# Attention and two expert layers on one core: the routing inside a unit takes one more step, row splits come later, weight splits of the remainder unit are spread anew

## The chip, the cores and the metric

The kernel runs on one core of a Trainium2 chip. The metric is the time of one execution in microseconds of device time. A measurement of the kernel is the median over several runs.

## The reference

Three parts follow each other. First attention over 4 batches, 12 heads, 448 rows of 64, with normalised queries and keys. Its output, 1,792 rows of 768, goes through two layers of eight experts. A row goes to the expert with the largest logit, and the expert's output is scaled by the softmax weight of that expert (in the first layer also by a sigmoid gate). The second layer adds a bias by the row's modality to the logits.

```python
logits = x @ w_gate + modality_bias[modality_id]      # layer 2; layer 1 has no bias
e_idx = np.argmax(logits, axis=1)
gate_w = softmax(logits)[rows, e_idx]
for e in range(8):
    h = np.maximum(x[e_idx == e] @ w1[e], 0.0)        # 768 to 1,024
    out[e_idx == e] = gate_w * (h @ w2[e])            # 1,024 to 768
```

## The kernel before, in words

Attention fills about the first 320 us. Then the two layers are done as a list of **units**. A unit is one expert with a group of the rows that were routed to it. In layer 1 there are a first unit `ua` (240 columns), the remainder unit `ub` (128 columns, the same expert) and then `P0` to `P6`, with room for 304, 288, 256, 240, 224, 208 and 192 rows. Layer 2 follows with `e2` and `e3` (304 rows each) and the smaller remainder groups.

Every value is kept as a high and a low half, so a product is three matmuls. A unit (`unit`, `halves`) has eight **first-layer steps**, each 18 matmuls into one PSUM buffer `pl`, of which there are three. After each, ACT writes the high half `hh` and VectorE the low half `hl` of the hidden block (line 377); the buffer is free for another step when `hl` is done. Beside them the weights of the second layer are split, `w2h` on ACT and `w2l` on VectorE (line 305). Then come six **second-layer steps** of 24 matmuls, which read `hh` and `hl`, and after each a transposition and the scaled rows `yr` on VectorE (line 436). In these the first-layer weights of the next unit are split (`w1h`, `w1l`).

The function `do(s)` is called at each step s of a unit (0 to 7 first layer, 7.5 between, 8 to 13 second layer) and does what is not matmul work:

- the **row splits** of the next unit, by the table `XPLAN`: "p" splits tile t of the gathered rows `xr` into `XS`, the high half on ACT (line 356) and the subtraction on GpSimd (line 357), "s" does the subtraction on VectorE, "t" is the transposing DMA on SyncE's queue;
- the fetch of rows for the unit after the next;
- one step of the **generator of the unit before** (`gen`): at step 0 its last transposition, the scatters of its rows `yr` to the table `yd` (one GpSimd DMA for each tile of 128 rows, line 382) and the logits' copy `lt`; at step 1 the logits `r_l` (line 489) for layer 2's routing and the routing itself up to the one-hot rows `rt_ohb` (line 112), two steps later the rank matmuls `rk` (lines 121 to 124), one step later the rest of the routing;
- side work from a dictionary, such as the weight splits for `P0` in `ub`.

Each engine works through its instructions in the order in which they are written. The scatters of a unit to `yd` wait for each other: the second is issued when the first has landed.

Of the kernel before, what the change touches and what calls it, by code (L numbers as in the profile page):

```python
# [9 lines left out]
NT=1792; D=768; F=1024; E=8; KD=6; KF=8  # L10
# [17 lines left out]
class Moe:  # L28
# [60 lines left out]
    def apart(self,i,key):  # L89
        i=getattr(i,"ins",i)  # L90
        self.tc.declare_no_dep(i,group=key,reason="a token has one place: the scatters write different rows"); self.tc.add_to_no_dep_group(key,i)
    def route_g(self, sp, psp, l, nt, R, ohsum, ordt, tokf=None, valid=None, og=None, mod=None, tag="sm", pay=None, iv=None, fine=0, apart=None):

        nc=self.nc; V=nc.vector
        T=lambda n,s=(),dt=F32: sp.tile([128,nt,*s],dt,name="rt_"+n,tag="rt_"+n)[:R]
        m=T("m"); V.tensor_reduce(m,l,axis=AX.X,op=ALU.max)
        if fine: yield
        d=T("d",(E,)); V.tensor_tensor(out=d,in0=l,in1=bc(m.unsqueeze(2),[R,nt,E]),op=ALU.subtract)
        ex=T("ex",(E,)); nc.scalar.activation(ex,d,AF.Exp)
        if fine: yield  # L100
        v=T("v",(E,)); V.scalar_tensor_tensor(out=v,in0=d,scalar=0.0,in1=bc(self.e8m[:R].unsqueeze(1),[R,nt,E]),op0=ALU.is_ge,op1=ALU.mult)
        if fine: yield
        mn=T("mn"); V.tensor_reduce(mn,v,axis=AX.X,op=ALU.min)
        if fine: yield
        s=T("s"); V.tensor_reduce(s,ex,axis=AX.X,op=ALU.add)
        if fine: yield
        oh=T("oh",(E,)); V.tensor_tensor(out=oh,in0=bc(self.e8m[:R].unsqueeze(1),[R,nt,E]),in1=bc(mn.unsqueeze(2),[R,nt,E]),op=ALU.is_equal)
        if fine: yield
        if valid is not None:
            V.tensor_tensor(out=oh,in0=oh,in1=bc(valid.unsqueeze(2),[R,nt,E]),op=ALU.mult)  # L110
            if fine: yield
        ohb=T("ohb",(E,),BF16); V.tensor_copy(ohb,oh)
        if fine:
            yield
            smx=T("smx",(E,))[:,0]; V.tensor_reduce(smx,oh.rearrange("p t e -> p e t"),axis=AX.X,op=ALU.add)
            rk=(yield "rk").rearrange("p (t e) -> p t e",t=nt)
        else:
            yield
            yield
            rk=psp.tile([128,nt,E],F32,name="rk",tag=tag)[:R]  # L120
        nc.tensor.matmul(rk,self.ones[:R,:R],bc(ohsum[:R].unsqueeze(1),[R,nt,E]),start=True,stop=False)
        for t in range(nt-1):
            nc.tensor.matmul(rk[:,t+1:],self.ones[:R,:R],bc(ohb[:,t:t+1],[R,nt-1-t,E]),start=False,stop=False)
        nc.tensor.matmul(rk,self.tri[:R,:R],ohb,start=False,stop=True)
# [12 lines left out]
        V.tensor_tensor(out=r,in0=r,in1=oh,op=ALU.mult)
        if fine: yield
        ix=T("ix"); V.tensor_reduce(ix,r,axis=AX.X,op=ALU.add)
        if fine: yield  # L140
        ixi=T("ixi",(),I32)
        if iv is None and valid is not None: iv=T("iv"); V.tensor_scalar(iv,valid,-BIG,BIG,op0=ALU.mult,op1=ALU.add)
        if iv is not None: V.tensor_tensor(out=ixi,in0=ix,in1=iv,op=ALU.add)
        else: V.tensor_copy(ixi,ix)
        if fine: yield
        if pay is None:
            pay=T("pay",(PW,)); nc.gpsimd.memset(pay[:,:,2:4],0.0)
            V.tensor_copy(pay[:,:,0],tokf)
            if mod is not None: V.tensor_copy(pay[:,:,2],mod)
        den=T("den"); V.tensor_scalar(den,s,1e-9,None,op0=ALU.add)  # L150
        if fine: yield
        if og is not None:
            V.scalar_tensor_tensor(out=den,in0=eo,scalar=1.0,in1=den,op0=ALU.add,op1=ALU.mult)
            if fine: yield
        V.reciprocal(pay[:,:,1],den)
        for t in range(nt):
            if fine: yield "sc"
            i=nc.gpsimd.indirect_dma_start(out=ordt[:,:],out_offset=bass.IndirectOffsetOnAxis(ap=ixi[:,t:t+1],axis=0),in_=pay[:,t,:],in_offset=None,bounds_check=E*NT-1,oob_is_err=False)
            if apart is not None: self.apart(i,apart); self.places.append(getattr(i,"ins",i).name)
# [109 lines left out]
    def alloc_rows(self,st,NM):  # L269
        nc=self.nc; ntl=(NM+127)//128; self.NM=NM; self.ntl=ntl  # L270
        self.XT=st.tile([128,2,KD,NM],F16,name="XT"); self.xh=self.XT[:,0]; self.xl=self.XT[:,1].bitcast(BF16)
        self.XS=st.tile([128,ntl,2,D],F16,name="XS")
        self.xr=[st.tile([128,D],F32,name=f"xr{t}") for t in range(ntl)]
        self.pays=[st.tile([128,ntl,PW],F32,name=f"pay{i}") for i in range(4)]
        self.idxs=[st.tile([128,ntl],I32,name=f"idx{i}") for i in range(4)]
        self.post=None; self.slot=0; self.turn=0; self.places=[]
    def clear_rows(self,j):
        for p in [self.xr[j]]+(self.pays if j==0 else []): self.nc.gpsimd.memset(p,0.0)
# [63 lines left out]
    def fetch_idx(self,u):  # L342
        nc=self.nc; ntl=u.ntl; pay=self.pays[u.slot]; idx=self.idxs[u.slot]
        v=self.lp.tile([128,self.ntl],F32,name="fv")[:,:ntl]
        nc.vector.tensor_scalar(v,self.pos3[:,:ntl],u.ent.cnt[:,u.g:u.g+1],None,op0=ALU.is_lt)
        nc.vector.scalar_tensor_tensor(out=v,in0=pay[:,:ntl,0],scalar=float(-NT),in1=v,op0=ALU.add,op1=ALU.mult)
        nc.vector.tensor_scalar(idx[:,:ntl],v,float(NT),None,op0=ALU.add)
    def gather(self,u,t=None):
        nc=self.nc; ntl=u.ntl; idx=self.idxs[u.slot]
# [122 lines left out]
    def warm2(self,db,eng):  # L472
        for k in ((0,1),(2,),(3,),(4,),(5,),())[db]: self.split_w1(k,eng=eng if k in (1,3) else None)
    def route2(self, u, scale):
        nc=self.nc; R=128; nx=u.L.nxt; sp=self.lp; sm=self.sm; ntl=u.ntl; yt=self.yt; pay=self.pays[u.slot][:,:ntl]; idx=self.idxs[u.slot][:,:ntl]
        nc.scalar.copy(self.lt[:2*E,:u.N],self.lgp[:2*E,:u.N])
        yield
        lg=sm.tile([128,ntl,E],F32,name="lg2",tag="tp")
        for t in range(ntl): nc.tensor.matmul(lg[:,t,:],self.lt[:2*E,ts(t,128)],self.fold[:2*E],start=True,stop=True)
        T=lambda n,s=(),dt=F32: sp.tile([128,self.ntl,*s],dt,name="r2_"+n,tag="r2_"+n)[:,:ntl]  # L480
        l=T("l",(E,)); b=T("b",(E,)); b2=T("b2",(E,)); nm=T("nm"); v=T("v"); tok=T("tok")
        sh=[128,ntl,E]
        nc.vector.tensor_copy(tok,idx)
        nc.vector.tensor_scalar(v,tok,float(NT),None,op0=ALU.is_lt)
        nc.vector.tensor_scalar(nm,pay[:,:,2],-1.0,1.0,op0=ALU.mult,op1=ALU.add)
        nc.vector.tensor_tensor(out=b,in0=bc(nx["bias"][:,0:1,:],sh),in1=bc(nm.unsqueeze(2),sh),op=ALU.mult)
        nc.vector.tensor_tensor(out=b2,in0=bc(nx["bias"][:,1:2,:],sh),in1=bc(pay[:,:,2:3],sh),op=ALU.mult)
        nc.vector.tensor_tensor(out=b,in0=b,in1=b2,op=ALU.add)
        nc.vector.tensor_tensor(out=l,in0=lg,in1=bc(scale,sh),op=ALU.mult)
        nc.vector.tensor_tensor(out=l,in0=l,in1=b,op=ALU.add)  # L490
        yield from self.route_g(sp,sm,l,ntl,R,nx["ohsum"],nx["ord"],tok,valid=v,tag="tp")

XPLAN={5:{0:[("p",2)],1:[("t",0),("t",1),("t",2)]},7:{9:[("s",0),("t",0)]},4:{0:[("p",0)],2:[("t",0),("t",1),("t",2)]},6:{1:[("t",0),("t",1),("t",2)]},0:{0:[("p",0),("p",1),("p",2)],7.5:[("t",0),("t",1),("t",2)]},3:{3:[("s",0)],4:[("s",1)],5:[("s",2)],7.5:[("t",0),("t",1),("t",2)]},
1:{8:[("s",0),("s",1),("s",2),("t",0),("t",1),("t",2)]},
    2:{7.5:[("s",0),("s",1),("s",2),("t",0),("t",1),("t",2)]},None:{10:[("s",0),("t",0)]}}
class LazyUnit:
# [329 lines left out]
def body_full(tc,q,k,v,g_q,g_k,wg,wog,w1,w2,mod,wg2,bias2,v1,v2,out,stop=False,O=None):  # L826
    nc=tc.nc
    with ExitStack() as ctx:
# [8 lines left out]
        S={}  # L837
# [113 lines left out]
                next(S[name],None)  # L951
            return f
        def xp(t): return lambda: M.xsplit(S["P"][0],t,nc.gpsimd)
        def w1(k): return lambda: M.split_w1(k,u=S["P"][0])
        M.unit(ua,nx=LazyUnit(S,"ub",same=True),fx=LazyUnit(S,"P",0),side={0:[tail0,step],1:[step,step],2:[step],5:[tail2],6:[tail3],7.5:[lambda: M.fetch_rows(S["ub"])],12:[xp(0)],13:[xp(1)]},late=7,fp=7,fr=9)
        P=S["P"]
        M.unit(S["ub"],nx=P[0],fx=P[1],side={j:[w1(k)] for k,j in enumerate((2,3,4,5,8,9))},late=5,fr=9)
        off2=cst.tile([128,E],F32,name="of2")
        def pick2():
            yield from M.pick_g("p2",lp,tp,c2,N2,tag="tp")  # L960
# [7 lines left out]
        S["B"]=[Unit(L2,be,g,N2) for g in range(G2)]; S["S"]=[Unit(L2,se,g,NS,x=True) for g in range(2)]  # L968
        B0=S["B"][0]
        P+=[LazyUnit(S,"e2"),LazyUnit(S,"e3")]  # L970
        sides={1:{KF+j:[stepper("table1")] for j in range(6)},2:{5:[stepper("pick2")]*2,**{j:[stepper("pick2")] for j in range(6,14)}},3:{5:[stepper("pick3")]*2,**{j:[stepper("pick3")] for j in range(6,14)}}}
        for g in range(7): M.unit(P[g],nx=P[g+1],fx=P[g+2],side=sides.get(g),late=0 if g else 3)
        e2,e3=S["e2"],S["e3"]
        def cold(u): M.fetch(u); M.cold(u); M.xall(u)
# [87 lines left out]
```

## Time and profile before

| what | value |
|---|---|
| runs shown, median (lowest to highest) | 886.72 us (885.95 to 888.47), 3 runs |
| profiled execution, its own time | 888.97 us |
| its span | 887.2 us |
| mean granted PE clock | 0.973 of full |
| PE, VectorE, ACT, GpSimd busy | 823.5, 674.9, 525.8, 389.9 us |

Busy shares are means over the whole span; attention and the two layers have different limits. The profiled execution is one run, 2.25 us over the median of the runs shown.

### The profile page before, as it was taken

To read this page: it belongs to the slowest core of one execution; us is meant where nothing else is said; L and a number is where in the kernel's file an instruction comes from. 1 tells how busy PE (TensorE), PEld (TensorE's weight loads), DVE (VectorE), ACT (ScalarE), POOL (GpSimd) and SP (SyncE) were. 2 spreads that over 40 slices of the span, in tenths; PEclk is the share of its full clock that TensorE was granted. 3 is DMA by queue.
4 is the path that set the end of the run, shared out by engine and by line. 5 is a ranking of instruction groups with operands and counts; after the bars stand their busy time and mean duration, and the time that the engine had idled before them with its cause. 6 is when DMAs were issued, how large, how long until landed. Compare 5 with 4: busy or idle time off the path is not lost. (4 is left out here: it accounts for less than half of the span.)

```text
span 887.2 us, 23322 instructions
## 1 busy us (share of the span) xinstructions
PE 823.5 (93%) x8881; PEld 644.0 (73%) x8898; DVE 674.9 (76%) x1414; ACT 525.8 (59%) x967; POOL 389.9 (44%) x409
## 2 busy tenths in 40 slices
PE   4699999999999799799999999989999999989996
PEld 1365666666665588677889899889777778867775
DVE  6689889888878775775788888888775768558865
ACT  4577777776766653555555656666445545437653
POOL 5686777876776523420514333433402424023202
PEclk9799999999999899999999999999999999999999
DMA  5577666765565383959495797797778776967941
GB/s 135 128 159 192 153 157 159 198 158 155 130 172 127 124 238 84 332 196 279 144 323 146 271 302 190 265 347 166 268 243 288 233 187 250 279 211 237 346 158 51
DMA packets 142138, 181.44 MB, mean 204 GB/s; under 512 B 71944, under 2 KB 109592, under 8 KB 142016
## 3 DMA queue, kind: packets, MB, share of 16 engines
q1 hardware_dynamic: 134048, 157.06, 60.3%
q0 software_dynamic: 6656, 22.32, 7.9%
q8 instruction: 72, 1.18, 0.6%
q10 hardware_dynamic: 1312, 0.47, 0.2%
q14 instruction: 50, 0.41, 0.1%
HBM read 129.73 MB, written 23.94 MB: 173 GB/s over the span
## 5 line engine op out<-in xcount | busy, mean ns | idle before, releaser
L373 PE MATMUL pl<-XT,w1h 128*128 128x304 f16 (+6 forms) x1236 | 209.4, 274 | 2.9 <-DVEq L1012 1.8
L373 PE MATMUL pl<-hh,w2h 128*128 128x304 f16 (+7 forms) x720 | 195.7, 276 | 0.1
L373 PE MATMUL pl<-hh,w2l 128*128 128x304 f16 (+7 forms) x720 | 195.3, 275 | 0.0
L373 PE MATMUL pl<-hl,w2h 128*128 128x0 bf16 x720 | 189.3, 265 | 1.6 <-DVE hl L377 1.6
L373 PE MATMUL pl<-XT,w1l 128*128 128x304 f16 (+6 forms) x618 | 172.1, 279 | 0.7 <-issue 0.6
L672 POOL TENSOR_TENSOR plo<-p 128x448 f16<-128x448 f32 x142 | 139.4, 1000 | 55.4 <-ACT p L669 52.0
L373 PEld LDWEIGHTS <-w1h 128*128 128x128 f16 x1536 | 135.9, 98 | 31.6 <-issue 8.7
L373 PEld LDWEIGHTS <-w2h 128*128 128x128 f16 x1440 | 135.2, 98 | 24.7 <-issue 1.6
L305 DVE TENSOR_TENSOR w1l<-r,w1h 128x1024 bf16<-128x1024 f32 x90 | 109.4, 1231 | 37.5 <-ACT w1h L304 35.3
L357 POOL TENSOR_TENSOR XS<-xr,XS 128x768 bf16<-128x768 f32 (+5 forms) x30 | 52.9, 1780 | 152.7 <-ACT XS L356 141.6
L445 ACT COPY yt<-pl 128x304 f32<-128x304 f32 (+8 forms) x102 | 36.5, 357 | 131.0 <-PE pl L373 130.8
L669 ACT ACTIVATE p<-pst,eb 128x896 f32<-128x896 f32 (+1 forms) x96 | 86.5, 911 | 14.9 <-PE pst L665 14.2
L304 ACT CAST w1h<-r 128x1024 f16<-128x1024 f32 x90 | 93.3, 1054 | 0.1
L376 ACT ACTIVATE hh<-pl 128x304 f16<-128x304 f32 (+8 forms) x135 | 49.1, 366 | 74.6 <-PE pl L373 68.6
L682 PE MATMUL av<-vv,p 128*128 128x65 f16 (+1 forms) x768 | 89.8, 199 | 2.0 <-ACT xrow L694 2.0
L682 PEld LDWEIGHTS <-p 128*128 128x128 bf16 (+1 forms) x768 | 73.5, 102 | 21.3 <-issue 15.3
L684 PE MATMUL av<-vv,plo 128*128 128x65 f16 (+1 forms) x768 | 87.9, 196 | 0.8 <-DVE plo L672 0.8
L683 PE MATMUL av<-vv,p 128*128 128x64 f16 (+1 forms) x768 | 88.4, 198 | 0.0
L373 PEld LDWEIGHTS <-w1l 128*128 128x128 bf16 x768 | 75.2, 99 | 12.6 <-issue 0.9
L646 DVE TENSOR_REDUCE m<-psm 128x2 f16<-128x896 f32 x70 | 76.0, 1086 | 9.6 <-PE psm L641 7.9
L373 PEld LDWEIGHTS <-w2l 128*128 128x128 bf16 x720 | 70.9, 98 | 15.0 <-issue 2.3
L683 PEld LDWEIGHTS <-p 128*128 128x128 bf16 (+1 forms) x768 | 74.7, 103 | 2.0 <-issue 1.0
(331 smaller groups left out, 1798.2 us busy)
## 6 DMA issues: line engine op xcount, KB each, us to landing
r<-in_moe_w_dram SPq DMA_DIRECT2D x96, 512.0 KB, 8.9
raw<-in_moe_w_dram SPq DMA_DIRECT2D x64, 384.0 KB, 6.9
r2a<-in_moe_w_dram SPq DMA_DIRECT2D x32, 384.0 KB, 7.5
r2b<-in_moe_w_dram SPq DMA_DIRECT2D x32, 384.0 KB, 8.1
T<-Z SPq DMA_DIRECT2D x48, 224.0 KB, 4.1
T<-Z SPq DMA_DIRECT2D x48, 112.0 KB, 3.0
yd<-zero SPq DMA_DIRECT2D x14, 384.0 KB, 3.1
rv<-in_v_dram SPq DMA_DIRECT2D x24, 192.0 KB, 3.8
```

The source lines that it names most:

```text
L304: if part!=1: nc.scalar.copy(h,t)
L305: if part!=0: (eng or nc.vector).tensor_tensor(out=l,in0=t,in1=h,op=ALU.subtract)
L357: if part!=0: (eng or nc.vector).tensor_tensor(out=self.XS[:m,t,1].bitcast(BF16),in0=x,in1=h,op=ALU.subtract)
L373: self.nc.tensor.matmul(o,a,b,start=i==0,stop=i==tot-1); i+=1
L376: nc.scalar.activation(h,p,AF.Relu)
L445: nc.scalar.copy(self.yt[:,db,:N],p)
L646: if t<3: nc.vector.tensor_reduce(m[:,t:t+4:3],p[:,:,:S],axis=AX.X,op=ALU.max,negate=True)
L669: self.nc.scalar.activation(self.d["P",i][:,self.u(kt)],p[:,:nn,:S],AF.Exp,bias=self.eb,scale=0.125)
L672: eng.tensor_tensor(out=self.d["L",i][:,u],in0=P[:,u],in1=self.hi(P)[:,u],op=ALU.subtract)
L682: nc.tensor.matmul(o,hh,w[:,0:65],start=kt==0,stop=False)
L683: nc.tensor.matmul(o[:,0:64],hh,w[:,65:129],start=False,stop=False)
L684: nc.tensor.matmul(o,ll,w[:,0:65],start=False,stop=kt==3)
```

## The change

The routing of a unit's rows for layer 2 (`route2`) gets a step of its own between the logits and the routing, so that the logits are at step 1, the one-hot rows at step 2, the rank matmuls at step 4 and the rest at step 5, one later than before. With `lag` the exponential on ACT comes a step after the one-hot rows and its sum after the rank matmuls. A small tile `val` keeps which of a unit's places are in use, so that `r_tok` and `r_v` need not be worked out again.

In `XPLAN` entry 0 (units P1 to P6, e2 and the first remainder groups of layer 2) the three row splits move from step 0 to steps 1, 2 and 3. In entry 5 (`ub`) the second and the third split are on VectorE at steps 1 and 2, and one is taken out of `ua`'s step 13. The weight splits of `P0` inside `ub` are at steps 3, 4, 8, 9, 10, 11 in place of 2, 3, 4, 5, 8, 9, and the first two subtract on GpSimd.

```diff
-    def route_g(self, sp, psp, l, nt, R, ohsum, ordt, tokf=None, valid=None, og=None, mod=None, tag="sm", pay=None, iv=None, fine=0, apart=None):
+    def route_g(self, sp, psp, l, nt, R, ohsum, ordt, tokf=None, valid=None, og=None, mod=None, tag="sm", pay=None, iv=None, fine=0, apart=None, lag=False):
...
-        ex=T("ex",(E,)); nc.scalar.activation(ex,d,AF.Exp)
+        ex=T("ex",(E,)); s=T("s")
+        if not lag: nc.scalar.activation(ex,d,AF.Exp)
...
-        s=T("s"); V.tensor_reduce(s,ex,axis=AX.X,op=ALU.add)
+        if not lag: V.tensor_reduce(s,ex,axis=AX.X,op=ALU.add)
...
         else:
             yield
+            if lag: nc.scalar.activation(ex,d,AF.Exp)
             yield
             rk=psp.tile([128,nt,E],F32,name="rk",tag=tag)[:R]
...
         yield "r"
+        if lag: V.tensor_reduce(s,ex,axis=AX.X,op=ALU.add)
...
+        self.vals=[st.tile([128,ntl],F32,name=f"val{i}") for i in range(4)]
...
-        nc.vector.tensor_scalar(v,self.pos3[:,:ntl],u.ent.cnt[:,u.g:u.g+1],None,op0=ALU.is_lt)
-        nc.vector.scalar_tensor_tensor(out=v,in0=pay[:,:ntl,0],scalar=float(-NT),in1=v,op0=ALU.add,op1=ALU.mult)
+        val=self.vals[u.slot][:,:ntl]
+        nc.vector.tensor_scalar(val,self.pos3[:,:ntl],u.ent.cnt[:,u.g:u.g+1],None,op0=ALU.is_lt)
+        nc.vector.scalar_tensor_tensor(out=v,in0=pay[:,:ntl,0],scalar=float(-NT),in1=val,op0=ALU.add,op1=ALU.mult)
...
-        nc.vector.tensor_copy(tok,idx)
-        nc.vector.tensor_scalar(v,tok,float(NT),None,op0=ALU.is_lt)
...
-        yield from self.route_g(sp,sm,l,ntl,R,nx["ohsum"],nx["ord"],tok,valid=v,tag="tp")
...
+        yield
+        yield from self.route_g(sp,sm,l,ntl,R,nx["ohsum"],nx["ord"],pay[:,:,0],valid=v,tag="tp",lag=True)
...
-XPLAN={5:{0:[("p",2)],1:[("t",0),("t",1),("t",2)]},7:{9:[("s",0),("t",0)]},4:{0:[("p",0)],2:[("t",0),("t",1),("t",2)]},6:{1:[("t",0),("t",1),("t",2)]},0:{0:[("p",0),("p",1),("p",2)],7.5:[("t",0),("t",1),("t",2)]},3:{3:[("s",0)],4:[("s",1)],5:[("s",2)],7.5:[("t",0),("t",1),("t",2)]},
+XPLAN={5:{1:[("s",1),("t",0)],2:[("s",2),("t",1)],3:[("t",2)]},7:{9:[("s",0),("t",0)]},4:{0:[("p",0)],2:[("t",0),("t",1),("t",2)]},6:{1:[("t",0),("t",1),("t",2)]},0:{1:[("p",0)],2:[("p",1)],3:[("p",2)],7.5:[("t",0),("t",1),("t",2)]},3:{3:[("s",0)],4:[("s",1)],5:[("s",2)],7.5:[("t",0),("t",1),("t",2)]},
...
-        def w1(k): return lambda: M.split_w1(k,u=S["P"][0])
-        M.unit(ua,nx=LazyUnit(S,"ub",same=True),fx=LazyUnit(S,"P",0),side={0:[tail0,step],1:[step,step],2:[step],5:[tail2],6:[tail3],7.5:[lambda: M.fetch_rows(S["ub"])],12:[xp(0)],13:[xp(1)]},late=7,fp=7,fr=9)
+        def w1(k): return lambda: M.split_w1(k,eng=nc.gpsimd if k<2 else None,u=S["P"][0])
+        M.unit(ua,nx=LazyUnit(S,"ub",same=True),fx=LazyUnit(S,"P",0),side={0:[tail0,step],1:[step,step],2:[step],5:[tail2],6:[tail3],7.5:[lambda: M.fetch_rows(S["ub"])],12:[xp(0)]},late=7,fp=7,fr=9)
...
-        M.unit(S["ub"],nx=P[0],fx=P[1],side={j:[w1(k)] for k,j in enumerate((2,3,4,5,8,9))},late=5,fr=9)
+        M.unit(S["ub"],nx=P[0],fx=P[1],side={j:[w1(k)] for k,j in enumerate((3,4,8,9,10,11))},late=5,fr=9)
...
-        sides={1:{KF+j:[stepper("table1")] for j in range(6)},2:{5:[stepper("pick2")]*2,**{j:[stepper("pick2")] for j in range(6,14)}},3:{5:[stepper("pick3")]*2,**{j:[stepper("pick3")] for j in range(6,14)}}}
+        sides={1:{KF+j:[stepper("table1")] for j in range(6)},2:{6:[stepper("pick2")]*2,**{j:[stepper("pick2")] for j in range(7,14)}},3:{6:[stepper("pick3")]*2,**{j:[stepper("pick3")] for j in range(7,14)}}}
```

What it moves, in the order of the engines. GpSimd, in P4 (the row splits `XS` of P5's rows, the scatters `yd<-yr` of P3's rows, then the routing's table entries), before:

```order
L357 TENSOR_TENSOR XS<-xr_78,XS 128x768
L357 TENSOR_TENSOR XS<-xr_79,XS 80x768
L382 DMA yd<-yr,idx_86 1792x768 x2
L147 MEMSET rt_pay 128x2x2
L158 DMA o_1128<-rt_pay,rt_ixi 14720x4 x2
L352 DMA xr_78<-xd,idx_85 128x768
```

and of the change:

```order
L387 DMA yd<-yr,idx_86 1792x768 x2
L362 TENSOR_TENSOR XS<-xr_78,XS 128x768
L362 TENSOR_TENSOR XS<-xr_79,XS 80x768
L150 MEMSET rt_pay 128x2x2
L161 DMA o_1132<-rt_pay,rt_ixi 14720x4 x2
L357 DMA xr_78<-xd,idx_85 128x768
```

The two splits stood ahead of the two scatters and now stand behind both; the rest is in its old place.

VectorE, in P4 from the first hidden block to the one after the one-hot rows, before (the row splits don't appear, they are GpSimd's):

```order
L489 TENSOR_TENSOR r_l<-lg_9151,pay_82 128x16
L490 TENSOR_TENSOR r_l<-r_l,r_b 128x16
L96 TENSOR_REDUCE rt_m<-r_l 128x2
L98 TENSOR_TENSOR rt_d<-r_l,rt_m 128x16
L101 SCALAR_TENSOR_TENSOR rt_v<-rt_d,e8m 128x16
L103 TENSOR_REDUCE rt_mn<-rt_v 128x2
L105 TENSOR_REDUCE rt_s<-rt_ex 128x2
L107 TENSOR_TENSOR rt_oh<-e8m,rt_mn 128x16
L110 TENSOR_TENSOR rt_oh<-rt_oh,r_v 128x16
L112 CAST rt_ohb<-rt_oh 128x16
L377 SCALAR_TENSOR_TENSOR hl<-pl_9132,hh 128x224
L305 TENSOR_TENSOR w2l<-raw_115,w2h 128x768
```

and of the change:

```order
L492 TENSOR_TENSOR r_l<-lg_9133,pay_82 128x16
L493 TENSOR_TENSOR r_l<-r_l,r_b 128x16
L382 SCALAR_TENSOR_TENSOR hl<-pl_9112,hh 128x224
L309 TENSOR_TENSOR w2l<-raw_119,w2h 128x768
L96 TENSOR_REDUCE rt_m<-r_l 128x2
L98 TENSOR_TENSOR rt_d<-r_l,rt_m 128x16
L102 SCALAR_TENSOR_TENSOR rt_v<-rt_d,e8m 128x16
L104 TENSOR_REDUCE rt_mn<-rt_v 128x2
L108 TENSOR_TENSOR rt_oh<-e8m,rt_mn 128x16
L111 TENSOR_TENSOR rt_oh<-rt_oh,val_90 128x16
L113 CAST rt_ohb<-rt_oh 128x16
L382 SCALAR_TENSOR_TENSOR hl<-pl_9150,hh 128x224
```

A hidden block `hl` and a weight split `w2l` now lie between the logits `r_l` and the maximum `rt_m`; the sum `rt_s` has left this place.

GpSimd in ub (row splits of P0's rows, scatters of ua's rows, weight splits `wxl` for P0), before:

```order
L357 TENSOR_TENSOR XS<-xr_78,XS 128x768
L357 TENSOR_TENSOR XS<-xr_79,XS 128x768
L357 TENSOR_TENSOR XS<-xr_80,XS 48x768
L382 DMA yd<-yr,idx_85 1792x768 x2
L147 MEMSET rt_pay 128x2x2
```

and of the change:

```order
L362 TENSOR_TENSOR XS<-xr_78,XS 128x768
L387 DMA yd<-yr,idx_85 1792x768 x2
L309 TENSOR_TENSOR wxl<-r_0_70,wxh 128x1024
L309 TENSOR_TENSOR wxl<-r_1_71,wxh 128x1024
L150 MEMSET rt_pay 128x2x2
```

Two row splits have left GpSimd, and two weight splits stand behind the scatters.

## Rows read from the trace of the kernel before

**Rows 1.** Idle time of PE from 300 us to the end, by what ended it.

```profile
PE pl L373 <- DVE hl L377: 8.4, 11, 1.8
PE rk L123 <- DVE rt_ohb L112: 5.9, 6, 1.5
...
PE rk L121 <- DVE r_l L489: 1.7, 2, 1.3
```

**Rows 2.** Timeline of PE in P4: start, length, work, idle before it.

```profile
534.11 0.17 PE L121 MATMUL rk<-c,ones 128*128 128x16 bf16 x1
535.12 0.17 PE L123 MATMUL rk<-rt_ohb,ones 128*128 128x8 bf16 x1 [0.84 <-DVE rt_ohb L112]
...
535.41 0.34 PE L373 MATMUL pl<-XT,w1h 128*128 128x224 f16 x2
...
541.97 0.26 PE L373 MATMUL pl<-hh,w2h 128*128 128x224 f16 x1
```

**Rows 3.** Timeline of VectorE in P4, same columns.

```profile
530.25 2.21 DVE L305 TENSOR_TENSOR w2l<-raw,w2h 128x768 bf16<-128x768 f32 x1 [0.33 <-DMA r<-in_moe_w_dram]
532.38 0.15 DVE L483 CAST r_tok<-idx 128x2 f32<-128x2 int32 x1
...
532.65 0.16 DVE L485 TENSOR_SCALAR r_nm<-pay 128x2 f32<-128x2 f32 x1
...
535.27 0.95 DVE L305 TENSOR_TENSOR w2l<-raw,w2h 128x768 bf16<-128x768 f32 x1
...
543.68 0.39 DVE L377 SCALAR_TENSOR_TENSOR hl<-pl,hh 128x224 bf16<-128x224 f32 x1
```

**Rows 4.** Timeline of GpSimd in P4.

```profile
528.37 3.27 POOL L357 TENSOR_TENSOR XS<-xr,XS 128x768 bf16<-128x768 f32 x2 [13.42 <-ACT XS L356]
531.80 1.55 POOL L382 DMA_INDIRECT yd<-yr,idx  x1 [0.16 <-issue]
537.36 0.97 POOL L382 DMA_INDIRECT yd<-yr,idx  x1 [4.01 <-DMA yd<-yr,idx]
```

**Rows 5.** Timeline of VectorE in P5.

```profile
560.47 0.38 DVE L377 SCALAR_TENSOR_TENSOR hl<-pl,hh 128x208 bf16<-128x208 f32 x1 [0.63 <-ACT hh L376]
561.19 2.23 DVE L305 TENSOR_TENSOR w2l<-raw,w2h 128x768 bf16<-128x768 f32 x1 [0.35 <-ACT w2h L304]
```

**Rows 6.** Timeline of GpSimd in P5.

```profile
559.33 3.28 POOL L357 TENSOR_TENSOR XS<-xr,XS 128x768 bf16<-128x768 f32 x2 [9.98 <-DMA r2b<-in_moe_w_dram]
562.77 1.55 POOL L382 DMA_INDIRECT yd<-yr,idx  x1 [0.16 <-issue]
569.68 0.94 POOL L382 DMA_INDIRECT yd<-yr,idx  x1 [5.36 <-DMA pay<-o]
```

**Rows 7.** Timeline of VectorE from P2 to P3.

```profile
463.57 1.93 DVE L305 TENSOR_TENSOR w2l<-raw,w2h 128x768 bf16<-128x768 f32 x1 [0.30 <-ACT w2h L304]
...
477.56 0.42 DVE L377 SCALAR_TENSOR_TENSOR hl<-pl,hh 128x256 bf16<-128x256 f32 x1
...
497.86 2.18 DVE L305 TENSOR_TENSOR w2l<-raw,w2h 128x768 bf16<-128x768 f32 x1 [0.31 <-ACT w2h L304]
```

**Rows 8.** PE in P2: the eighth block of the first second-layer step.

```profile
478.60 0.27 PE L373 MATMUL pl<-hh,w2h 128*128 128x256 f16 x1
```

**Rows 9.** Timeline of PE in P6.

```profile
597.88 0.17 PE L123 MATMUL rk<-rt_ohb,ones 128*128 128x8 bf16 x1 [1.49 <-DVE rt_ohb L112]
```

**Rows 10.** A stretch of P6: length, busy us of five engines, granted clock, DMA.

```profile
597.90:601.20 3.30, 3.24 (x22) 3.04 (x22) 3.30 (x7) 2.01 (x6) 0.00 (x0) 0.50 0.31 119
```

**Rows 11.** Timeline of VectorE in P6.

```profile
593.63 1.60 DVE L483 CAST r_tok<-idx 128x2 f32<-128x2 int32 x1
```

**Rows 12.** Timeline of PE in ub.

```profile
362.95 0.17 PE L123 MATMUL rk<-rt_ohb,ones 128*128 128x8 bf16 x1 [1.50 <-DVE rt_ohb L112]
...
369.91 0.27 PE L373 MATMUL pl<-hh,w2h 128*128 128x128 f16 x1
```

**Rows 13.** Timeline of GpSimd in ub.

```profile
366.31 0.99 POOL L382 DMA_INDIRECT yd<-yr,idx  x1 [4.85 <-DVE c L128]
```

More of the change, by code (lines that the diff above doesn't have):

```diff
@@ L474, in route2 @@
     def route2(self, u, scale):
-        nc=self.nc; R=128; nx=u.L.nxt; sp=self.lp; sm=self.sm; ntl=u.ntl; yt=self.yt; pay=self.pays[u.slot][:,:ntl]; idx=self.idxs[u.slot][:,:ntl]
+        nc=self.nc; R=128; nx=u.L.nxt; sp=self.lp; sm=self.sm; ntl=u.ntl; yt=self.yt; pay=self.pays[u.slot][:,:ntl]; v=self.vals[u.slot][:,:ntl]
         nc.scalar.copy(self.lt[:2*E,:u.N],self.lgp[:2*E,:u.N])
@@ L480, in route2 @@
         T=lambda n,s=(),dt=F32: sp.tile([128,self.ntl,*s],dt,name="r2_"+n,tag="r2_"+n)[:,:ntl]
-        l=T("l",(E,)); b=T("b",(E,)); b2=T("b2",(E,)); nm=T("nm"); v=T("v"); tok=T("tok")
+        l=T("l",(E,)); b=T("b",(E,)); b2=T("b2",(E,)); nm=T("nm")
         sh=[128,ntl,E]
-        nc.vector.tensor_copy(tok,idx)
-        nc.vector.tensor_scalar(v,tok,float(NT),None,op0=ALU.is_lt)
         nc.vector.tensor_scalar(nm,pay[:,:,2],-1.0,1.0,op0=ALU.mult,op1=ALU.add)
```

## Prediction

> **What bounds the kernel now.** I read the page first, then the waits of PE over the two expert layers, then, unit by unit, the timelines of PE, VectorE and GpSimd. PE is the engine that decides: in the whole stretch from 300 us on it is idle in a handful of places, and three lines hold nearly all of what this change can touch [rows 1]. It waits 8.4 us in 11 places for the low half of the hidden block (hl, which frees a PSUM buffer and feeds the second layer), 5.9 us in 6 places for the one-hot rows of the routing (rt_ohb) and 1.7 us in 2 places for the logits (r_l). So the gain on offer is the 7.6 us of the last two, plus what they cause; the question is what ends last once they are gone.
>
> P4 shows it. PE issues the first rank matmul at 534.11, must then wait 0.84 us for rt_ohb, resumes its steps at 535.41, and starts the second layer at 541.97 [rows 2]. The four steps between take 6.56 us, 1.64 each, for 18 matmuls; a second-layer step has 24, so about 2.19. Its eighth and last block, the one that reads hl(7), starts 7/8 of that later, at 543.88, and the hl matmul is one matmul further, about 543.97. VectorE ends hl(7) at 543.68 + 0.39 = 544.07 [rows 3]. So PE needs hl(7) within 0.1 us of when VectorE has it: **behind the routing wait stands VectorE's own queue, with no slack**. That PE no longer waits for rt_ohb lets it arrive 0.84 us sooner at a result that is not ready sooner.
>
> What fills VectorE's queue? Eight pairs of hl and w2l, the routing, and one disturbed operation: the w2l at 530.25 took 2.21 us, the one at 535.27 took 0.95 [rows 3]. It ran while GpSimd worked on the row splits XS (528.37, two in 3.27 us, 1.64 each) [rows 4]. P5 tells the same: w2l at 561.19 took 2.23 us while the second XS ran (559.33 to 562.61), but the hl at 560.47, in the middle of the splits, took only 0.38, since one of its operands is in PSUM [rows 5, 6]. So a VectorE operation with both inputs in SBUF stands still while GpSimd subtracts; one that reads PSUM doesn't.
>
> **The change, part by part.** *The two operations r_tok and r_v* go: from 532.38 to the start of r_nm at 532.65, 0.27 us of VectorE per unit [rows 3]. *The step more of the routing:* the logits are worked at step 1, the one-hot rows at step 2, the exponential at step 3, the rank matmuls at step 4. PE then asks for rt_ohb 1.64 us later; on VectorE an hl and a w2l (1.3 us) go ahead of it, but the stalled 1.26 us of the w2l before and the 0.27 fall away. The wait for it in P3 to P5 (about 2.9: the 5.9 less 1.5 each in P6 and ub, which come below) falls to nothing or nearly. The exponential on ACT and the sum of it on VectorE are as long as before. That is the gain, on PE.
>
> *The row splits*, steps 1, 2, 3 in place of 0, are the cost. By the order of GpSimd they stood ahead of the unit's scatters and now stand behind them. The second scatter waits for the first to land: 531.80 to 537.36 in P4, 5.56 us [rows 4], and 6.91 in P5 [rows 6]. Freed of the splits, the first scatter can start between 528.37 and 531.80, so the second starts between 533.9 and 537.4, lasts 1.0, and the two splits follow until 538.2 to 541.6. All of that lies between the fourth step and hl(7), where VectorE has no free time, while today half of the splits lies in the tail of the unit before. The price of one split there: GpSimd holds 1.64 us, in which VectorE can do one hl (0.3 to 0.39) and no w2l, so 1.3 us. Bounds: 0.65 if the two engines mix well enough that half is lost, 1.64 if nothing goes beside it.
>
> By the Trainium skill ("SBUF — State Buffer", section "Who interferes with whom") a VectorE instruction with two SBUF inputs contends with a GpSimd instruction that reads SBUF, whoever issues first blocks the other for its whole length, and reductions never contend. The 2.21 and 2.23 agree with it, and the 0.38 too. If the lock held back the small routing operations in full as well, by 1.64 each, the sum below would be 0.7 higher in each of P3 to P5, 893.3 in all; it speaks against this change.
>
> So in P4 VectorE's hl(7) moves by -(2.21 - 0.95) - 0.27 + 2 x 1.3 = +1.1 us (bounds -0.2 and +1.8), and with it PE. P5: -1.28 - 0.27 + 2.6 = +1.05, taken as 1.1. P3: its w2l took 2.18 [rows 7], so +1.1. P2 has three scatters ahead of its two splits; its w2l took 1.93, so hl(7), now done at 477.56 + 0.42 = 477.98, moves by +1.35; the block that needs it starts at 478.60 and its hl matmul some 0.1 later, so 0.7 us of the move is slack and +0.6 to 0.7 remains [rows 7, 8]. P1 has 288 columns for P2's 256, so more slack: +0.1. e2 and the remainder units after it have 304 columns: 0.
>
> P6 is split both ways. Its waits for r_l and rt_ohb are the longest of their lines, 1.3 and 1.5 us, the second until 597.88 [rows 1, 9], and right behind them PE ran at half clock, 0.50 granted from 597.9 to 601.2 [rows 10], that is 1.2 GHz for 3.3 us, or 1.65 us lost. What delayed them is a cast, r_tok, that took 1.60 us beside a split, where P4's took 0.15, and that now is gone [rows 3, 11]. All that back would be -4.45. But the unit prepares e2, three splits: VectorE gets 3 x 1.3 = 3.9 more, less 1.60 + 0.12 for the two removed operations: +2.2, and if PE, now early, stalls in one piece its clock can fall again. With what PE gets back and VectorE loses in one unit I take +1.2, about half of +2.2, bounds -4.5 and +3.9 (2.2 and another 1.65 for the clock).
>
> *ub, the remainder unit:* the splits of its next rows go from GpSimd to VectorE, two of about 0.95 (the w2l of that shape [rows 3]); the weight splits 0 and 1 go from VectorE to GpSimd, the others into the second layer. That takes four weight splits (about 1.27 each, 0.95 by 1024/768) out of VectorE's way. PE waits in ub 1.5 us for rt_ohb and starts the second layer at 369.91 [rows 12]; at best all of that wait and as much again for hl behind it goes, about 3.2 us. Against it: the two weight splits stand on GpSimd behind ua's second scatter, for which GpSimd is idle 4.85 us [rows 13]; each takes, estimated from 1.64 by 1024/768 columns, 2.2 us, and would hold the last routing operations, of which the second layer's hl come next. Then it is +0.3. I take -0.8, nearer to the second.
>
> Sum: 0.1 + 0.7 + 1.1 + 1.1 + 1.1 + 1.2 - 0.8 = **+4.5 us**. The profiled run took 888.97 us (span 887.2), so it would be 893.5; the median of the runs shown is 886.72, 2.25 below it, so I forecast 891.2. About 0.3%, 2.7 us, is what a measurement here can tell from no change.
>
> **The rivals.** *The splits cost half* (0.65 each): -0.2 in each of P3 to P5, 0 in P2, about +0.5 in P6, ub -0.8: some 886 to 887, no change. For it: the two engines take turns when both have work, so a GpSimd split can lie where VectorE has only PSUM reads; against it both w2l beside a split took over twice their time. *New stalls drop PE's clock:* two or three of P2 to P6 with a stall over a microsecond in one piece and then 3.3 us at 1.2 GHz, 1.65 each: 894.5 to 896. For it: P6; against it: the mean granted clock of the whole run is 0.973, so such falls are few. *Faster:* the splits come after hl(7) and cost nothing on VectorE. Then P3 to P5 give 2.9, P6 4.45, ub 0.8: 8.2 us, 878.5. It decides at the landing of the first scatter: in P4 the splits are out of the way if the second scatter starts after about 542, a landing of 10 us or more, where 5.6 to 6.9 are measured. That the change doesn't do what it says, the wait for rt_ohb merely becoming one for hl, is my own case.
>
> **How the numbers follow.** My forecast 0.50 (of it 0.04 below 2.7 us), the clock 0.13, half cost 0.20, faster 0.17. So slower 0.59, same 0.24, faster 0.17. The range 884.5 to 897 holds the first three and leaves most of the faster case out; the likeliest one's own is 888.5 to 893.5.
>
> **What would show it.** The wait of rk for rt_ohb gone or under 0.3 in P3 to P6; XS on GpSimd behind the second scatter, in steps 4 to 7; in those steps w2l of 1.6 to 2.3 us; PE waiting 1 to 2 us for hl around the second layer's first step in P2 to P6; ub's second layer starting less than 1.5 us sooner; P6 at full clock or not. I am wrong if XS starts after hl(7), if w2l beside XS keeps its 0.95, or if ub's second layer starts 3 us sooner.

## The result and the profile after

The changed kernel took 899.26 us (median of 6 runs, 895.29 to 903.29) where the kernel before took 887.6 us (6 runs, 885.95 to 892.94). The ratio is 1.0121 with a 95% interval of 1.0088 to 1.0153: slower, by 10.7 us of 887.6 (7.8 to 13.6; the two medians differ by 11.7). The forecast was slower by 4.5 us. The profiled run is the longest of the six, 903.29 us with a span of 901.5.

First the waits of PE from 300 us on, as in [rows 1].

```profile
PE pl L378 <- DVE hl L382: 19.0, 14, 5.0
PE cps L166 <- DVE c L131: 4.5, 2, 2.9
PE lgT L446 <- DVE yl L453: 2.3, 1, 2.3
...
PE rk L125 <- DVE rt_ohb L113: 1.5, 2, 1.2
```

The waits that were to go are gone: the 5.9 us for rt_ohb are 1.5, the 1.7 us for r_l are none. In their place the wait for hl grew from 8.4 to 19.0 us, its longest from 1.8 to 5.0. The wait for the count `c` (line 131, part of the routing's last operations) is new, and the one for `yl` in the remainder unit grew from 0.5 to 2.3. Where hl is late is seen in P4 on VectorE, whose rows answer to [rows 3].

```profile
539.98 0.38 DVE L382 SCALAR_TENSOR_TENSOR hl<-pl,hh 128x224 bf16<-128x224 f32 x1
540.38 4.62 DVE L309 TENSOR_TENSOR w2l<-r2a,w2h 128x768 bf16<-128x768 f32 x1
544.92 0.16 DVE L128 TENSOR_REDUCE rt_s<-rt_ex 128x2 f32<-128x16 f32 x1
...
546.19 0.37 DVE L382 SCALAR_TENSOR_TENSOR hl<-pl,hh 128x224 bf16<-128x224 f32 x1
...
547.34 0.38 DVE L382 SCALAR_TENSOR_TENSOR hl<-pl,hh 128x224 bf16<-128x224 f32 x1
```

One w2l, a matter of 0.95 us, took 4.62. Everything behind it on VectorE, the last eleven routing operations and three hl, came 3.67 us later. GpSimd in the same stretch, for [rows 4]:

```profile
532.54 1.01 POOL L387 DMA_INDIRECT yd<-yr,idx  x1 [11.31 <-DVE yr L441]
539.54 1.37 POOL L387 DMA_INDIRECT yd<-yr,idx  x1 [5.99 <-DMA pay<-o]
540.93 3.24 POOL L362 TENSOR_TENSOR XS<-xr,XS 128x768 bf16<-128x768 f32 x2
```

The order is the one that was forecast: the second scatter waits for the landing of the first (7.0 us here), then come both splits, with nothing between, 540.93 to 544.17. The w2l began in the tail of the scatter, 0.55 us ahead of the first split, and ended 0.83 us after the second, nearly its own length of 0.95. So it made next to no way beside either. PE in P4, for [rows 2]:

```profile
539.07 0.17 PE L123 MATMUL rk<-c,ones 128*128 128x16 bf16 x1
539.10 0.17 PE L125 MATMUL rk<-rt_ohb,ones 128*128 128x8 bf16 x1
...
546.61 0.26 PE L378 MATMUL pl<-hh,w2h 128*128 128x224 f16 x1 [2.38 <-DVE hl L382]
```

The rank matmul for rt_ohb follows the first at once, 0.03 us, where it waited 0.84. Seven and a half microseconds later the second layer waits 2.38 us for hl.

P6 shows it with three splits and with a far smaller operation: `c`, 8 numbers a row, which takes 0.17 us elsewhere; the longest wait of PE, 5.0 us, is the one for the hl behind it. First VectorE, then GpSimd.

```profile
606.83 5.51 DVE L131 TENSOR_TENSOR c<-c,rt_smx 128x8 bf16<-128x8 bf16 x1
612.27 0.16 DVE L140 TENSOR_TENSOR rt_r<-rt_r,rt_oh 128x16 f32<-128x16 f32 x1
```

```profile
606.19 1.28 POOL L387 DMA_INDIRECT yd<-yr,idx  x1 [6.55 <-DMA yd<-yr,idx]
607.48 4.83 POOL L362 TENSOR_TENSOR XS<-xr,XS 128x768 bf16<-128x768 f32 x3
```

The same stands in B0 and B1, the two remainder units of layer 2 that follow e3, which I had written off as having slack: in B0 a w2l, in B1 a comparison of one number a row.

```profile
722.34 6.09 DVE L309 TENSOR_TENSOR w2l<-r2a,w2h 128x768 bf16<-128x768 f32 x1 [0.24 <-ACT w2h L308]
...
756.53 5.32 DVE L1005 TENSOR_TENSOR over<-ova,s1ni 128x1 int32<-128x1 f32 x1
```

And four stretches of PE at half clock, 0.50 to 0.56 granted, in or right behind such a stall, in P4, P5, P6 and the remainder unit, where before there was one in ub (369.2 to 372.5, 0.50) and the one of [rows 10] (columns as there).

```profile
547.40:550.70 3.30, 3.30 (x21) 2.81 (x20) 1.95 (x7) 0.18 (x1) 0.90 (x1) 0.51 0.93 151
578.00:581.80 3.80, 3.80 (x28) 3.39 (x26) 3.70 (x16) 0.34 (x1) 1.16 (x1) 0.56 0.00 0
612.50:618.50 6.00, 4.94 (x32) 4.73 (x32) 4.02 (x15) 0.97 (x3) 1.20 (x1) 0.50 1.04 222
373.40:376.60 3.20, 3.20 (x39) 3.02 (x38) 3.20 (x7) 1.38 (x3) 0.00 (x0) 0.51 1.03 400
```

The lengths of the units, from the first matmul of one to the first of the next, read from the timeline of PE of each kernel's profile (us; left out are P1, e2 and e3, which differ by at most 1.6 between the profiles, and what follows B1, where the small unit S0 takes 15.4 to 17.8 us in a stretch that none of the edits touches):

| unit | before | after | E1 | E2 | E4 | E5 | E6 | E7 | E9 |
|---|---|---|---|---|---|---|---|---|---|
| ub | 24.9 | 22.6 | 24.6 | 24.9 | 22.0 | 25.2 | 23.0 | 20.1 | 20.6 |
| P0 | 39.9 | 39.9 | 40.0 | 39.9 | 42.7 | 39.9 | 39.9 | 39.9 | 39.9 |
| P2 | 34.6 | 36.6 | 34.6 | 36.3 | 34.6 | 34.6 | 35.2 | 34.6 | 34.6 |
| P3 | 32.4 | 35.1 | 32.2 | 36.7 | 32.4 | 32.4 | 34.7 | 32.0 | 32.4 |
| P4 | 31.0 | 33.8 | 30.6 | 35.1 | 31.0 | 30.9 | 33.0 | 30.6 | 31.3 |
| P5 | 30.3 | 32.0 | 29.9 | 33.4 | 31.2 | 30.0 | 32.0 | 29.9 | 30.3 |
| P6 | 31.5 | 34.3 | 30.7 | 36.8 | 31.0 | 30.1 | 32.7 | 30.5 | 31.3 |
| B0 | 39.2 | 40.3 | 39.2 | 40.3 | 39.2 | 39.2 | 39.2 | 39.2 | 39.2 |
| B1 | 35.8 | 37.9 | 35.8 | 37.9 | 35.8 | 35.8 | 37.9 | 35.8 | 35.8 |

Between the two profiles P2 to P6 lose 12.0 us, B0 and B1 3.2, and ub gains 2.3.

### The profile page after: what moved, and what is told of

Read it like the earlier page. It is cut to its first block, busy times and chain, and to the rows that moved or that the text cites. A ratio compares the mean times of both kernels' runs of the same rounds, so it can differ in the third digit from the quotient of the medians.

```text
span 901.5 us, 23308 instructions
## 1 busy us (share of the span) xinstructions
PE 826.5 (92%) x8881; PEld 645.7 (72%) x8898; DVE 695.3 (77%) x1396; ACT 526.9 (58%) x967; POOL 390.0 (43%) x409
## 5 line engine op out<-in xcount | busy, mean ns | idle before, releaser
L378 PE MATMUL pl<-hh,w2h 128*128 128x304 f16 (+7 forms) x720 | 198.3, 280 | 8.5 <-DVE hl L382 8.5
L378 PE MATMUL pl<-hh,w2l 128*128 128x304 f16 (+7 forms) x720 | 197.7, 279 | 0.0
L378 PE MATMUL pl<-hl,w2h 128*128 128x0 bf16 x720 | 191.6, 268 | 2.0 <-DVE hl L382 1.9
L378 PEld LDWEIGHTS <-w2h 128*128 128x128 f16 x1440 | 137.4, 100 | 34.1 <-issue 10.5
L688 PEld LDWEIGHTS <-plo 128*128 128x128 f16 (+1 forms) x768 | 74.7, 104 | 0.8 <-DVE plo L676 0.8
```

The costliest lines, as they stand in the source:

```text
L378: self.nc.tensor.matmul(o,a,b,start=i==0,stop=i==tot-1); i+=1
L688: nc.tensor.matmul(o,ll,w[:,0:65],start=False,stop=kt==3)
```

## The experiments

Two theories stood at the start. **Q**: a row of GpSimd splits holds one VectorE operation for its whole length, and with it hl, which waits behind it in VectorE's queue. **R**: the routing's later steps put its last operations before hl(7) and delay it. Others came with the later runs. Of long code lines the diffs show the changed pieces alone.

**E1, row splits back at step 0**, all else of the change kept.

```diff
-0:{1:[("p",0)],2:[("p",1)],3:[("p",2)],7.5:
+0:{0:[("p",0),("p",1),("p",2)],7.5:
```

> The changed kernel with one thing undone: the three row splits of each unit are back at step 0, ahead of the scatters. Theory Q (two or three GpSimd splits in a row hold one VectorE operation for their whole length, and hl waits behind it): the single VectorE operations of 3.9 to 6.1 us in P1 to P6 and B0, B1 vanish, and 12 to 16 us of the changed kernel's time with them: 882 to 886 us, below the kernel before, as the remainder unit's gain stays. Rival R (the routing's later steps delay the last operations before hl(7)): 895 or more.

Measured: 0.9936 of the kernel before (0.9906 to 0.9966), 5.7 us faster, about 881.9 on the scale of 887.6. P2 to P6, B0 and B1 have their old lengths or less. Moving the splits costs 1.0121 less 0.9936, 1.9% or 16 us (12 to 20, the two intervals taken together); R has fallen. PE's waits from 400 to 800 us:

```profile
PE pl L378 <- DVE hl L382: 4.5, 5, 1.5
...
PE rk L125 <- DVE rt_ohb L113: 1.0, 2, 0.6
```

hl still takes 4.5 us here: it is what stands next.

**E2, the late row splits alone**, on the kernel before (the edit of E1 the other way).

> The kernel before with one thing of the change: row splits at steps 1, 2, 3. Theory Q: slower than before by 10 to 15 us, 898 to 903, with single VectorE operations of 4 to 6 us. Rival R: no change, 886 to 889.

Measured: 1.0282 (1.0222 to 1.0342), more than expected. P3 on VectorE and on PE:

```profile
502.09 4.71 DVE L305 TENSOR_TENSOR w2l<-r2a,w2h 128x768 bf16<-128x768 f32 x1
```

```profile
507.13 0.19 PE L163 MATMUL cps<-c,ones 128*128 128x8 bf16 x1 [3.79 <-DVE c L128]
```

The held w2l takes 4.71 us, as P3's does in the changed kernel. With the old routing the count `c` and the matmul that sums it for the next group's choice stand right behind it, and PE waits 3.79 us in the middle of its first layer. So the late splits cost more without the later routing than with it; that this is the whole of the difference to E1's 16 us I have not shown.

**E3, the later routing alone** (E1 and the remainder unit as before).

> The kernel before with the routing's later steps alone (row splits at step 0, the remainder unit as before). Theory Q: faster by 2 to 6 us, 882 to 886, since the waits of the rank matmuls for the one-hot rows go and hl is next by little. Rival R: slower by 5 us or more.

Measured: 0.998 (0.9953 to 1.0007), 1.8 us faster, which can't be told from no change and is a little less than Q expected; R is out by it too. Its profile says where the gain went; the waits from 400 to 800 us:

```profile
PE pl L378 <- DVE hl L382: 4.6, 5, 1.5
...
PE rk L125 <- DVE rt_ohb L113: 1.0, 2, 0.6
```

In that stretch PE waited 4.0 us for rt_ohb before and waits 1.0 now, and for hl 0.6 before and 4.6 now. In P3, P4 and P5 the first layer is 0.9 us shorter and the second 0.4 to 0.7 longer.

**E4, the remainder unit's part alone**, on the kernel before (with it goes the row split in ua's step 13, which the diff leaves out).

```diff
-5:{0:[("p",2)],1:[("t",0),("t",1),("t",2)]}
+5:{1:[("s",1),("t",0)],2:[("s",2),("t",1)],3:[("t",2)]}
...
-def w1(k): return lambda: M.split_w1(k,u=S["P"][0])
+def w1(k): return lambda: M.split_w1(k,eng=nc.gpsimd if k<2 else None,u=S["P"][0])
...
-enumerate((2,3,4,5,8,9))
+enumerate((3,4,8,9,10,11))
```

> The kernel before with the remainder unit's part alone (its row splits on VectorE at steps 1 and 2, two weight splits on GpSimd behind the scatters, the rest in the second layer). From the two traces, where the remainder unit became 2.3 us shorter: faster by 1 to 3 us, 885 to 887. Rival: with the routing a step earlier the two VectorE row splits delay the one-hot rows, and the gain is nothing or a loss of 1 us.

Measured: 1.0004 (0.9975 to 1.0032). The expectation was wrong; the rival had the number, but not for its reason: ub is 2.9 us shorter, and P0 behind it 2.8 longer. GpSimd, then PE at P0's start, then PE's clock there:

```profile
369.40 1.01 POOL L158 DMA_INDIRECT o<-rt_pay,rt_ixi  x1 [0.28 <-POOL rt_pay L147]
375.26 1.63 POOL L158 DMA_INDIRECT o<-rt_pay,rt_ixi  x1 [4.85 <-DMA o<-rt_pay,rt_ixi]
376.89 2.15 POOL L305 TENSOR_TENSOR wxl<-r,wxh 128x1024 bf16<-128x1024 f32 x1
```

```profile
379.10 0.44 PE L373 MATMUL pl<-XT,wxl 128*128 128x304 f16 x1 [1.02 <-POOL wxl L305]
```

```profile
379.40:382.60 3.20, 3.20 (x16) 2.09 (x14) 0.47 (x1) 0.00 (x0) 2.59 (x3) 0.51 1.15 348
```

The second weight split stands behind two scatters of the routing, which wait for each other (4.85 us). It ends at 379.04, P0 has begun and waits 1.02 us for it, and PE then runs 3.2 us at half clock.

**E5, the row splits on VectorE** at the steps of the change.

```diff
-0:{1:[("p",0)],2:[("p",1)],3:[("p",2)],7.5:
+0:{1:[("s",0)],2:[("s",1)],3:[("s",2)],7.5:
```

> The changed kernel, but the row splits of P1 to P6, e2, B0 and B1 subtract on VectorE (0.95 us each) in steps 1 to 3, none on GpSimd. Theory Q (VectorE stands still for the whole row of GpSimd splits: 3.7 us for two, 5.2 for three): VectorE pays 1.9 or 2.4 in place of that, so 1.8 to 2.8 us less in each of seven units: ratio to the kernel before 0.995 to 1.004, where the changed kernel has 1.012. Rival W (any added work on VectorE in the first layer costs as much as the blocked time): 1.008 or more.

Measured: 0.9972 (0.9953 to 0.9992). Two or three operations of 0.95 us more on VectorE, in the same steps, cost far less than leaving them to GpSimd there; W has fallen. (ub is as long as before for another reason, its weight splits on GpSimd, which come below.)

**E6, scatters that don't wait for each other**, so that nothing holds the splits up. Different rows are written, so the order of the scatters is free.

```diff
-            if u.own: self.apart(i,"rows")
+            self.apart(i,"rows")
```

> The changed kernel with the scatters of one unit not waiting for each other, so that the row splits run on GpSimd in steps 1 to 3, as the ACT halves come. Theory Q: VectorE still loses about 1.6 us to each split, in steps where it has no slack, and the one-hot rows come later: ratio 1.004 to 1.014. Rival L (the landing of the first scatter makes the splits late, and lateness is what costs): 0.994 to 1.000, as with the splits at step 0.

Measured: 1.0107 (1.0088 to 1.0127). The splits in P4 now run at 531.19, as the second scatter ends, and hold one of the routing's small operations, which take 0.17 us:

```profile
530.52 3.95 DVE L490 TENSOR_TENSOR r_b<-bs,pay 128x16 f32<-128x16 f32 x1
534.51 0.17 DVE L491 TENSOR_TENSOR r_b<-r_b,r_b 128x16 f32<-128x16 f32 x1
```

```profile
529.80 1.36 POOL L387 DMA_INDIRECT yd<-yr,idx  x1 [0.30 <-issue]
531.19 3.24 POOL L362 TENSOR_TENSOR XS<-xr,XS 128x768 bf16<-128x768 f32 x2
```

So it isn't the lateness behind the landing that costs: VectorE is held as long in the earlier step. L has fallen.

**E7, row splits at step 0 and P0's weight splits on VectorE** in ub's second layer, the rest of the change kept.

```diff
-def w1(k): return lambda: M.split_w1(k,eng=nc.gpsimd if k<2 else None,u=S["P"][0])
+def w1(k): return lambda: M.split_w1(k,u=S["P"][0])
...
-enumerate((3,4,8,9,10,11))
+enumerate((7.5,8,9,10,11,12))
```

(and E1's edit.)

> The changed kernel with the row splits back at step 0 and all six weight splits of P0 on VectorE in the remainder unit's second layer (7.5, 8 to 12), none on GpSimd. In the profile with the splits at step 0 the remainder unit's second layer was 3.9 us longer than before, beside a weight split of 4.95 us on VectorE. Theory Q: that goes, ratio 0.989 to 0.992 where the splits at step 0 alone had 0.9936. Rival: six splits fill VectorE there, and the second layer stays as long: 0.993 to 0.996.

Measured: 0.9913 (0.9891 to 0.9935), 7.7 us faster than the kernel before. ub takes 20.1 us for 24.9, P0 is as before, and nothing is left of the half clock there. This version beats both kernels.

**E8, the splits parted**: the first at step 1, the others at step 7.

```diff
-0:{1:[("p",0)],2:[("p",1)],3:[("p",2)],7.5:
+0:{1:[("p",0)],7:[("p",1),("p",2)],7.5:
```

> The changed kernel with the first row split at step 1 and the others at step 7, so that GpSimd's second split is not released when the first ends. Theory Q: in P3 to P5 one w2l of 4.6 us becomes two of some 2 to 3 us with one hl between, and the time falls by up to 3 us, 1.006 to 1.012. If the two engines took turns anyway, nothing changes: one w2l of 4 us or more, 1.012.

Measured: 1.0121 (1.0092 to 1.0151). In P4 the held w2l falls from 4.62 to 3.09 us, as one split is left in its way; the second split went past hl(7) into the second layer.

```profile
539.63 3.09 DVE L309 TENSOR_TENSOR w2l<-r2a,w2h 128x768 bf16<-128x768 f32 x1
```

```profile
540.24 1.65 POOL L362 TENSOR_TENSOR XS<-xr,XS 128x768 bf16<-128x768 f32 x1
...
550.11 1.79 POOL L362 TENSOR_TENSOR XS<-xr,XS 80x768 bf16<-80x768 f32 x1
```

So the first half of the expectation came true and the time didn't follow. P4, P5 and B1 gain (32.3, 29.8 and 35.8 us for 33.8, 32.0 and 37.9), P3 doesn't (35.1), ub loses 2.2 (24.8, see below), and P6 takes 34.1, with one PE wait of 4.64 us for hl. It isn't a split that holds this hl last: it stands in VectorE's queue behind `fv`, which waits for the landing of `pay`, the table entries of a later unit's rows.

```profile
609.88 0.16 DVE L351 SCALAR_TENSOR_TENSOR fv<-pay,val 128x3 f32<-128x3 f32 x1 [2.66 <-DMA pay<-o]
...
610.15 0.35 DVE L382 SCALAR_TENSOR_TENSOR hl<-pl,hh 128x192 bf16<-128x192 f32 x1
```

SyncE issued that fetch at 599.62, 8.5 us after P6's first matmul, where E1 issues it 3.4 us after. Ahead of it in SyncE's order stand the unit's weight loads, and ahead of those the transposes of P6's rows, the last of them issued at about 584.3, as the late split of 582.54 to 584.31 ends. So the late splits seem to have made a new wait by way of the transposes; this is read from the order and wasn't tried alone.

**E9, the remainder unit's part alone with all weight splits on VectorE** (E4 with E7's steps).

> The kernel before with the remainder unit's part alone, but all six weight splits of P0 on VectorE in its second layer. If the weight splits on GpSimd are what took the remainder unit's gain back (1.000 with them), this has 0.995 to 0.998, its first layer 3 us shorter and P0's first layer as before. Rival: the gain is lost at P0's start in any case, 0.999 to 1.001.

Measured: 0.993 (0.9905 to 0.9955), better than expected. ub is 4.3 us shorter and P0 as before; the profile's 4.3 us and the measured 6.2 (4.0 to 8.4) agree within the interval. The six splits take 1.22 us each and the second layer keeps its length:

```profile
367.32 1.23 DVE L305 TENSOR_TENSOR wxl<-r,wxh 128x1024 bf16<-128x1024 f32 x1 [0.64 <-ACT wxh L304]
...
375.33 1.22 DVE L305 TENSOR_TENSOR wxl<-r,wxh 128x1024 bf16<-128x1024 f32 x1
```

**E10, E7 with the third row split on VectorE**, which only P6, e2, B0 and B1 have: `0:{0:[("p",0),("p",1),("s",2)],7.5:`.

> The best kernel so far (row splits at step 0, weight splits of P0 on VectorE, ratio 0.991) with the third row split, which P6, e2, B0 and B1 alone have, on VectorE. If a row of three GpSimd splits still holds VectorE in P6 (PE gaps of 2.1 and 1.0 us there), P6 becomes some 1 to 2 us shorter, 0.989 to 0.990; if it is hidden at step 0, no change, 0.991.

Measured: 0.9909 (0.9878 to 0.9941), no change to E7. P6 is 0.6 us shorter and B0 0.4 longer.

## Why the forecast had the sign and missed the size

**The routing's wait** went as forecast, to nothing in P3 to P6, and so did what stood behind it: hl, from VectorE's queue (E3: 3.0 us of one wait gone, 4.0 of the other come). Alone it gives nothing that can be measured.

**The order on GpSimd** went as forecast: splits behind the second scatter, in the steps before hl(7).

**The step that failed is "The price of one split there: GpSimd holds 1.64 us, in which VectorE can do one hl (0.3 to 0.39) and no w2l, so 1.3 us."** It supposes that hl passes beside a split and that VectorE has its turn between two. Neither holds once an operation with both inputs in SBUF is at the head of VectorE's queue: it waits, hl behind it waits too though its own operand is in PSUM, and in P4 both splits went first. The price there was 4.62 - 0.95 = 3.67 us for two, not 2.6; in P6 5.51 - 0.17 = 5.34 for three, not 3.9; in B0 6.09 - 0.95 = 5.14. My bounds, 0.65 to 1.64 a split, left out the 1.7 to 1.8 of these three. The rest of the sum for P4 holds: with 3.67 it is -1.26 - 0.27 + 3.67 = +2.1, and hl(7) ended 17.63 us after the unit's first matmul before and 19.65 after, +2.0 for a forecast of +1.1. The estimate beside it, 1.64 a split with the small operations held in full, 893.3 in all, had the price more nearly; it stood with no chance of its own and was counted in P3 to P5 alone. The 2.21 us of [rows 3], from which I took the price, was a w2l that came 0.24 us into the second of two splits and so paid for one alone. I had read the row and not asked what it would be for an operation that comes ahead of the first.

The Trainium skill ("SBUF — State Buffer", section "Who interferes with whom") says that the two contend and that issue order decides who blocks; its section "Summary: rules for kernel authors" says that the second one to issue waits until the first finishes. The trace agrees on the block, but the w2l at 540.38 began ahead of both splits and waited for both, and so did the small operations in P6 and E6; by that rule, taken for the splits alone, they would have gone first. In P2 of the changed kernel a w2l began 0.17 us into the first of two splits and waited for the second too, ahead of which it would have gone by that rule:

```profile
470.46 3.90 DVE L309 TENSOR_TENSOR w2l<-r2a,w2h 128x768 bf16<-128x768 f32 x1 [0.30 <-ACT w2h L308]
```

```profile
470.29 3.25 POOL L362 TENSOR_TENSOR XS<-xr,XS 128x768 bf16<-128x768 f32 x2
```

**"e2 and the remainder units after it: 0"** was wrong for B0 (+1.1) and B1 (+2.1), which take three splits each. I had costed the slack of their steps against 3.9 us, not against one piece of 5. (The half-cost rival's own terms give 885.8, not 886 to 887; that changes nothing here.)

**The clock**, which I had as a rival with 0.13, came: half clock in or behind the stalls of P4, P5 and P6. By the rows above PE was busy 3.30, 3.80 and 4.94 us there at 0.51, 0.56 and 0.50 of its clock, so it lost 1.6, 1.7 and 2.5 us, 5.8 in all, where P6 alone lost 1.6 before. That is 4.1 us of the profile's loss, for which my sum had no term in P4 and P5. It doesn't simply add to the price: in P4 hl(7) came 2.0 us later and the unit became 2.8 us longer, 1.5 of them in the second layer, where the half clock lay. Nor does the length of a stall alone tell when it comes: in P3 PE waited 2.9 us for `c` and ran on at full clock (1.00 from 510.9 to 514.3), in E4 it waited 1.02 us and ran at half clock behind it.

**ub** gained 2.3 us in the profile pair, not 0.8: its first layer is 4.2 us shorter, so one of the signs of being wrong that I had set, a second layer 3 us sooner, came true. I had the weight splits on GpSimd hold the routing's last operations. They came later than that and held a weight split on VectorE in the second layer instead, then PE, which lost its clock:

```profile
366.08 0.99 POOL L387 DMA_INDIRECT yd<-yr,idx  x1 [6.91 <-DMA yd<-yr,idx]
367.07 4.24 POOL L309 TENSOR_TENSOR wxl<-r,wxh 128x1024 bf16<-128x1024 f32 x2
```

```profile
369.16 3.25 DVE L309 TENSOR_TENSOR wxl<-r,wxh 128x1024 bf16<-128x1024 f32 x1 [0.65 <-ACT wxh L308]
```

```profile
372.67 0.23 PE L446 MATMUL lgT<-yl,wgs 128*16 128x128 f32 x1 [2.33 <-DVE yl L453]
```

In E1 (24.6), E5 (25.2) and E8 (24.8), whose ub is the same, both GpSimd splits went ahead of that VectorE operation, 4.95 us long in E1, and nearly nothing of the gain was left; 2.3 is what one profile had. With the weight splits on VectorE (E7, E9) 4.3 to 4.8 us stay.

The terms as measured between the two profiles: P1 +0.2, P2 +2.0, P3 +2.7, P4 +2.8, P5 +1.7, P6 +2.8, B0 +1.1, B1 +2.1, ub -2.3: 13.1 us, against a forecast of 4.5 for the same sum. The after profile is 4.0 us above its median, the one of before 1.4 above its own; 13.1 less 2.6 is 10.5, near the 10.7 of the ratio, though where those 2.6 lie in the profile I can't say.

**What stays open.** When VectorE has its turn between two GpSimd operations: in the kernel before a w2l at 592.17 ran between the second and the third split of P6 (it took 1.53 us, the two splits together 3.96 in place of 3.27), in the changed kernel `c` waited for all three. In both the ACT halves of all three were done by then.

```profile
592.17 1.53 DVE L305 TENSOR_TENSOR w2l<-raw,w2h 128x768 bf16<-128x768 f32 x1 [0.36 <-ACT w2h L304]
```

The cases with the long wait began while a scatter was being issued on GpSimd, or just behind it, but that alone doesn't decide it. In P2 of E2 two splits begin at 467.22, right behind a scatter, and `c` begins 0.21 us into the first; it waits for that one alone, and the operation behind it for the second:

```profile
467.43 1.48 DVE L128 TENSOR_TENSOR c<-c,rt_smx 128x8 bf16<-128x8 bf16 x1
468.83 1.69 DVE L137 TENSOR_TENSOR rt_r<-rt_r,rt_oh 128x24 f32<-128x24 f32 x1
```

VectorE lost nearly the whole row there too, in two pieces.

## What to carry to other kernels

Put GpSimd work that reads SBUF where VectorE is idle or reads PSUM, not in VectorE's fullest steps, whether the table of steps puts it there (E6) or the landing of a DMA ahead of it. Where VectorE's queue holds operations with both inputs in SBUF, cost a row of such GpSimd operations at its full length, in one piece for whatever stands at the head of the queue, and add what waits behind that. Where VectorE has room for the work itself (0.95 us for a split that takes GpSimd 1.64), doing it there is cheaper than a GpSimd operation that is free only by the count of busy time (E5: 0.9972 for 1.0121; GpSimd at step 0, E1, had 0.9936).

## What was not expected of the hardware

An operation of 8 numbers a row on VectorE (0.17 us) took 5.51 us beside three GpSimd subtractions, and one of 16 numbers a row 3.95 us beside two (E6). The w2l of P4 ended 0.83 us after the last split, nearly its whole length of 0.95, though it began 0.55 us before the first split: beside the tail of the scatter's issue it seems to have done nothing either. From the start of a scatter to the start of the next, which waits for it, 5.56 us passed in P4 before and 7.00 after, with the same rows; after, the profile names another DMA (`pay`) as the last that this start waited for.
